# One joint run for the low-rank term of two groups, V0 in four quads, V loaded ahead of batch 1, and two x loads that wait for transposes

## The chip, the cores and the metric

The kernel runs on one core of a Trainium2 chip (trn2). The metric is the device time of one execution in microseconds. Three runs of the kernel before took 325.17, 325.19 and 325.78 us; their median is 325.19 us.

## The reference

The input x is (8, 4224, 192) in float32: 8 batches, 4224 positions, 192 channels. Two layers follow each other.

```
w   = softmax(weight)                       # 8 heads x 7 taps
y   = causal convolution of x with w        # 24 channels per head, 7 taps along the positions
h   = (y^T @ U @ V)^T                       # U: 4224 x 32, V: 32 x 4224, per batch
u   = y + h
out = u + relu(u @ w_ch1) @ w_ch2           # 192 -> 768 -> 192, per position
```

The product with U sums over all positions of a batch, so no position of a batch has its h before the batch's whole convolution is done.

## The kernel before

The 8 x 4224 positions are 264 tiles of 128, worked on in 33 **groups** of eight tiles. A batch has 33 tiles, so groups cross batches. The stages:

- **x loads.** `x_part` (L76) loads a quarter of a batch from GpSimd's queue (POOL in the profile) and converts it to bf16; `XP` (L84) names the quarters 0 to 3. Batch 0 comes in six pieces (`KP`, L86). x tiles have two buffers.
- **Convolution.** TensorE multiplies x with band matrices: `conv` (L355, matmuls L369) for batches 0 and 1, with the whole window in two halves, and `conv32` (L321, matmuls L339) for batches 2 to 7. The latter needs a shifted copy of x, `xb_sb` (one buffer), that POOL makes with the copies of `x_shift` (L286: L293, L295, L305). ACT and DVE evict the results to `y_sb` (L256, L258).
- **U.** `tt_mm` (L396, matmuls L402) forms y^T U; `tt_split` and `tt_sum` (L412, L425) bring the four partial sums together on all four row quarters, as `tt_sb`. For batch 0 the last tiles come in late by `tt_late` (L679, matmuls L682), which reads `U4_sb`, a copy that POOL makes (L701), and `tt_done` (L420) writes `tt_sb`.
- **h and u.** For groups from 2 on, `h_group` multiplies V with `tt_sb` (L457) and DVE adds y (L479) to `u_sb`; `transp` (L496) then transposes `u_sb` to `uT` with a DMA transpose on SP's queue (L498). `transp(3)` is held until the last matmul of the convolution of batch 1.
- **Groups 0 and 1** go without a DMA transpose: `yT_part` (L503, matmuls L509) transposes y on TensorE with the identity, straight into PSUM banks, and `hT_part` (L518, matmuls L524) adds h there, with `V0_sb` (32 rows, L132) as the moving operand; then ACT and DVE evict the banks to `uT` (L256, L258). h of group 0 comes first, then the rest of y^T of group 1, then its h.
- **The two layers.** `w1` (L542, matmuls L554) multiplies with `W1_sb`, with relu evictions on ACT (L568) and DVE (L570). `w2` (L577, matmuls L583) multiplies with `W2_sb`; DVE adds u (L592) and SP stores the result (L600).

Order of the work: the program is in the order in which it is written (`manual_schedule`), each engine takes its own instructions in that order, and waits for semaphores of the others. `SLOTS` (L619) is a list written out by hand: in each slot the W1 of some groups, then the pieces of W2 of some groups, with named steps at given pieces: `h3` (h of group 3, with its transpose), `d1` (convolution of batch 1), `c2:0:3:AAD` (three heads of the convolution of batch 2), `t1`/`s1` (the U product), `x2:6` (the six copies of `x_shift` for batch 2), `l2:3` (load of quarter 3 of batch 2, held until the last W2 piece issued so far). `LOADS` (L670) holds the other x loads until a given matmul of W1: `x_load` and `held` (L610, L602) add the wait. Since POOL is in order, what stands behind a held load on POOL waits with it. The built program gives POOL's loads eight semaphores in turn; a load waits until the load eight places before it on POOL has landed.

The order of POOL in the first 35 us: two x loads of batch 0, index patterns, U, two more x loads, V0, four loads of W1, quarter 0 of batch 1, the copy for `U4_sb`, five loads of V, W2, quarters 1 to 3 of batch 1, the copies for `band2`, then quarters 0 to 3 of batch 2.

Of the kernel before, what the change touches and what calls it, by code (L numbers as in the profile page):

```python
# [9 lines left out]
BF16 = mybir.dt.bfloat16  # L10
# [4 lines left out]
def kernel(  # L15
# [20 lines left out]
    GT = 8  # L36
# [3 lines left out]
    HB = P // 2  # L40
# [4 lines left out]
    cst = ctx.enter_context(tc.tile_pool(name="cst", bufs=1))  # L45
# [4 lines left out]
    uts = ctx.enter_context(tc.tile_pool(name="uts", bufs=5))  # L50
# [5 lines left out]
    def bank():  # L56
        return psp.tile([P, 512], F32, name="ps", tag="ps")
# [12 lines left out]
    def x_tile(b):  # L70
        xt[b] = xs.tile([P, NB1 + 1, D], BF16, name="x_sb")

    def x_zero(b, eng):
        eng.memzero(xt[b][0:HB, 0, :])

    def x_part(b, r, s0, s1):  # L76

        blk = NB0 * r + s0 - 1
        return nc.gpsimd.dma_start(  # L79
            out=xt[b][HB * r : HB * r + HB, s0:s1, :],  # L80
            in_=x[b, blk * HB : (blk + s1 - s0) * HB, :].rearrange("(j p) d -> p j d", p=HB),
        )

    XP = [(0, 1, 17), (0, 17, NB0 + 1), (1, 0, 18), (1, 18, NB1 + 1)]  # L84
# [18 lines left out]
    def iota(t, pattern, base, mul):  # L103
# [20 lines left out]
        out=Ur[:, 0:nfull, :], in_=U4[0 : nfull * P, :].rearrange("(k p) c -> p k c", p=P)  # L124
# [4 lines left out]
        x_piece(k)  # L129


    V0_sb = cst.tile([R, 2 * GT * P], BF16, name="V0_sb")  # L132
    nc.gpsimd.dma_start(out=V0_sb[:], in_=moe_V[:, 0 : 2 * GT * P])
    W1_sb = cst.tile([P, 3, M4], BF16, name="W1_sb")
    for m0, m1 in ((0, 2 * P), (2 * P, M4)):
        for hf in range(2):
            nc.gpsimd.dma_start(
                out=W1_sb[HB * hf : HB * hf + HB, :, m0:m1],
                in_=moe_w_ch1[:, m0:m1].rearrange("(c k) m -> k c m", k=HB),
# [27 lines left out]
    for hh in range(2):  # L167
# [3 lines left out]
        out=dif[:], in0=dif[:], scalar1=rq[:, 0:1], scalar2=None, op0=ALU.add  # L171
# [5 lines left out]
        out=d_sb[:],  # L177
# [8 lines left out]
        out=hot[:],  # L186
# [6 lines left out]
        out=ident[:], in0=fp[:], scalar1=float(P), scalar2=None, op0=ALU.is_equal  # L193
# [9 lines left out]
        out=c_sb[:].rearrange("p k h -> p h k"),  # L203
# [5 lines left out]
    for hh in range(2):  # L209
# [3 lines left out]
            out=pr[:],  # L213
# [8 lines left out]
        out=Eq[:], in0=efp[:], scalar1=rq[:, 1:2], scalar2=None, op0=ALU.is_equal  # L222
# [31 lines left out]
    def evac(eng, out, in_):  # L254
        if eng == "A":
            nc.scalar.activation(out=out, in_=in_, func=ACT.Copy)  # L256
        else:
            nc.vector.tensor_copy(out=out, in_=in_)  # L258
# [179 lines left out]
    uTt = [None] * NG  # L438
# [57 lines left out]
    def transp(g):  # L496
        uTt[g] = uts.tile([P, 4, 3, P], BF16, name="uT")
        return nc.sync.dma_start_transpose(  # L498
            out=uTt[g][:].rearrange("p i c t -> p (i c) t"),
            in_=ut[g][:].rearrange("p i c f k -> p (i c f k)"),  # L500
        )

    def yT_part(g, parts):  # L503


        for c, i0, i1, p, _ in parts:
            for i in range(i0, i1):
                for hf in range(2):
                    nc.tensor.matmul(  # L509
                        out=p[HB * hf : HB * hf + HB, (i - i0) * P : (i - i0 + 1) * P],  # L510
                        lhsT=yt[0][:, GT * g + 4 * hf + i, HB * c : HB * c + HB],
                        rhs=ident[:],
                        start=(i == i0),
                        stop=False,
                        tile_position=(0, HB * hf),
                    )

    def hT_part(g, parts):  # L518

        uTt[g] = uts.tile([P, 4, 3, P], BF16, name="uT")  # L520
        for c, i0, i1, p, _ in parts:
            for hf in range(2):
                t0 = (2 * g + hf) * 4 * P
                nc.tensor.matmul(  # L524
                    out=p[HB * hf : HB * hf + HB, 0 : (i1 - i0) * P],
                    lhsT=ttb[0][0:R, HB * c : HB * c + HB],
                    rhs=V0_sb[:, t0 + i0 * P : t0 + i1 * P],
                    start=False,
                    stop=True,
                    tile_position=(0, HB * hf),  # L530
                )
        for c, i0, i1, p, eng in parts:
            evac(
                eng,
                uTt[g][:, i0:i1, c, :],
                p[:, 0 : (i1 - i0) * P].rearrange("p (i t) -> p i t", t=P),
            )

    RELU = ["AD", "AD", "AA", "AD", "AD", "AD"]
    RELU0 = ["AA", "AD", "AA", "AD", "AA", "AD"]  # L540
# [77 lines left out]

    SLOTS = [  # L619
        ([0], [], {}),  # L620
        ([1], [0], {0: ["h0"], 1: ["h3", "l2:2"], 2: ["l2:3"]}),
        ([2], [1], {0: ["d1", "h1"], 1: ["t1"], 3: ["s1"], 4: ["h4", "x2:6"]}),
        ([3], [2], {1: ["h5"], 3: ["h6"]}),
        (
            [4, 5],
# [66 lines left out]
    work = [bank() for _ in range(4)]  # L692
    tp = bank()
    u_layout(work)
    x_tile(1)
    x_zero(1, nc.gpsimd)
    x_part(1, *XP[0])
    o = 0
    for r, (k0, k1) in KP[2].items():
        j = NB0 // 2 * r + k0  # L700
# [24 lines left out]
    W2_sb = cst.tile([P, MC, D], BF16, name="W2_sb")  # L725
    nc.gpsimd.dma_start(out=W2_sb[:], in_=moe_w_ch2[:].rearrange("(m p) d -> p m d", p=P))

    parts0 = [(0, 0, 2, bank(), "A"), (0, 2, 4, bank(), "D"), (1, 0, 4, bank(), "D")]
    yT_part(0, parts0)
    def conv_piece(k):  # L730
        for n, h in enumerate(range(0, H, 3)):
            for r in KP[k]:
# [6 lines left out]
    ps0 = work[3]  # L739
    for n, part in enumerate(ttb[0]):  # L740
        nc.tensor.matmul(out=ps0[:, 0:D], lhsT=R4[:], rhs=part[:], start=(n == 0), stop=False)
    more = [(2, 0, 2, bank(), "A"), (2, 2, 4, bank(), "A")]
    yT_part(0, more[0:1])
    tt_late(ps0)
    yT_part(0, more[1:])
    parts1 = [(0, 0, 4, bank(), "A")]
    yT_part(1, parts1)
    tt_done(0, ps0)
    hT_part(0, parts0 + more)
    rest = [(c, 0, 4, bank(), "ADA"[c]) for c in (1, 2)]  # L750
    yT_part(1, rest)
    hT_part(1, parts1 + rest)
    band2 = cst.tile([P, H, QB], BF16, name="band2")
    for xp in XP[1:]:
        x_part(1, *xp)
    for r in range(4):
        q = slice(QB * r, QB * r + QB)
# [6 lines left out]
    def do(what):  # L764
        if what[0] == "c":
            b, h0, n, engs = what[1:].split(":")
            conv32(int(b), int(h0), int(n), engs)
            return
        if what[0] == "d":
            for h in range(H):  # L770
                last = conv(int(what[1:]), h, 1, [0, 1], "AA" if h == 2 else "AD")
            held(transp(3), last)
            return
        if what[0] == "l":
            b, q = (int(v) for v in what[1:].split(":"))
            x_load(b, q, done_w2[-1])
            return
        if what[0] == "x":
            b, n = (int(v) for v in what[1:].split(":"))
            steps.extend(x_shift(b))  # L780
            for _ in range(n):
                steps.pop(0)()
            return
        n = int(what[1:])
        if what[0] == "h":
            h_group(n)
            if n > 1 and n != 3:
                transp(n)
        elif what[0] == "t":
            tt_split(n, tt_mm(n, range(NT)))  # L790
        else:
            tt_sum(n)
# [55 lines left out]
```

## Time and profile before

| | us |
|---|---|
| median of three runs | 325.19 |
| span of the profiled execution | 323.20 |
| PE busy | 317.6 |
| DVE busy | 268.6 |
| ACT busy | 170.0 |
| POOL busy | 142.7 |
| W1 of group 0 begins | 20.45 |
| W1 of groups 2 and 3 begins | 33.76, 47.12 |
| convolutions of batches 1, 2 and 3 begin | 37.75, 66.88, 95.08 |
| transposes of groups 2 and 3 issue | 27.14, 41.04 |

The span is the time from the first to the last instruction of the profiled execution; the median of the runs is 1.99 us above it. TensorE's granted clock is full from start to end. Times in the text are counted from the start of the span. A row of a timeline gives start, length, engine, line, operation and tiles, and in brackets how long the engine had been idle before it and what ended that. A row of the chain of waits gives start, length and what the chain ran through. "DMA to landing" is the time from the issue of a transfer to the semaphore that tells of its end; the three numbers are the least, the median and the most of the transfers asked for, and are equal for a single one.

### The profile page before, as it was taken

The page shows a single profiled execution, that of the slowest core. Times are in us where ns is not written, and L with a number is a line of the kernel's source. Part 1 is how long each engine was busy: PE and PEld are TensorE (multiplying, and loading weights), DVE is VectorE, ACT ScalarE, POOL GpSimd, SP SyncE. Part 2 cuts the span into 40 slices and gives each one's busy share as a digit, 9 for nine tenths or more (in the row PEclk, how much of TensorE's full clock was granted, in tenths as well). Part 3 has the DMA queues.
Part 4 walks back from the last instruction along what each step waited for, and adds up shares of the span by engine and source line. Part 5 has one row for each costly group of instructions (what it writes and reads, how often), then busy time and mean ns, then how long its engine had stood idle before and what let it go on. Part 6 is the DMA issues. An engine that isn't in the chain of part 4 may idle for free.

```text
span 323.2 us, 9583 instructions
## 1 busy us (share of the span) xinstructions
PE 317.6 (98%) x3996; PEld 223.7 (69%) x3996; DVE 268.6 (83%) x551; ACT 170.0 (53%) x344; POOL 142.7 (44%) x111
## 2 busy tenths in 40 slices
PE   8999999999999999999999999999999999999995
PEld 3747676478677647866864884687797497487495
DVE  6769989987977986997898699789888897896863
ACT  1766724860874397088239609824903902912910
POOL 8764179728957983992897497000000000000000
PEclk9999999999999999999999999999999999999999
DMA  9999993999998999599499957138268059048035
GB/s 106 192 191 183 206 209 100 196 192 257 208 135 200 246 142 190 166 189 209 130 237 192 181 149 194 52 105 231 61 178 262 3 150 275 18 121 271 2 121 173
DMA packets 122906, 53.51 MB, mean 166 GB/s; under 512 B 87760, under 2 KB 122832, under 8 KB 122864
## 3 DMA queue, kind: packets, MB, share of 16 engines
q1 hardware_dynamic: 84528, 38.08, 45.4%
q0 software_dynamic: 38192, 14.73, 39.2%
q8 instruction: 31, 0.51, 0.7%
q10 hardware_dynamic: 144, 0.10, 0.1%
q14 instruction: 11, 0.09, 0.1%
HBM read 29.49 MB, written 25.95 MB: 172 GB/s over the span
## 4 chain that ended last, share of the span: by engine, by line
PE 92%; ACT 3%; DMA 2%; DVE 1%; issue 0%; POOL 0%; POOLq 0%
PE ps L583 42%; PE ps L554 39%; PE ps L339 3%; PE ps L457 3%; DMA x_sb<-in_x_dram 2%; PE ps L402 2%; ACT rl_sb L568 2%; PE ps L369 1%; ACT y_sb L256 1%; PE ps L509 1%; DVE u_sb L479 1%; DVE rl_sb L570 1%; PE ps L524 0%; PE ps L428 0%; POOL x_sb L79 0%
## 5 line engine op out<-in xcount | busy, mean ns | idle before, releaser
L568 ACT ACTIVATE rl_sb<-ps 128x512 bf16<-128x512 f32 x233 | 124.3, 604 | 108.0 <-PE ps L554 96.0
L583 PE MATMUL ps<-W_sb,rl_sb 128*128 128x192 bf16 x1584 | 141.2, 246 | 0.2
L583 PEld LDWEIGHTS <-rl_sb 128*128 128x128 bf16 x1584 | 128.3, 98 | 11.8 <-issue 11.5
L554 PE MATMUL ps<-uT,W_sb 64*128 64x512 bf16 x1188 | 131.7, 376 | 0.0
L570 DVE TENSOR_SCALAR rl_sb<-ps 128x512 bf16<-128x512 f32 x163 | 105.3, 688 | 15.7 <-PE ps L554 15.4
L554 PEld LDWEIGHTS <-W_sb 64*128 64x128 bf16 x1188 | 66.9, 94 | 60.4 <-issue 3.9
L592 DVE TENSOR_TENSOR out_sb<-ps,u_sb 128x384 f32<-128x384 f32 (+1 forms) x133 | 70.4, 551 | 25.5 <-PE ps L583 25.0
L305 POOL COPY xb_sb<-x_sb 32x3072 bf16<-32x3072 bf16 (+1 forms) x24 | 67.4, 2824 | 0.5
L479 DVE TENSOR_TENSOR u_sb<-y_sb,ps 128x192 bf16<-128x192 bf16 (+1 forms) x168 | 66.3, 461 | 0.0
L293 POOL COPY xb_sb<-x_sb 128x3072 bf16<-128x3072 bf16 x12 | 32.7, 2742 | 42.1 <-PE ps L339 32.2
L256 ACT ACTIVATE y_sb<-ps 128x384 bf16<-128x384 f32 (+4 forms) x90 | 38.3, 520 | 9.7 <-PE ps L339 7.4
L79 POOL DMA_DIRECT2D x_sb<-in_x_dram x32 | 27.0, 848 | 9.6 <-PE ps L457 3.8
L258 DVE CAST y_sb<-ps 128x408 bf16<-128x408 f32 (+4 forms) x36 | 19.1, 578 | 1.3 <-PE ps L369 1.0
L457 PE MATMUL ps<-tt_sb,V_sb 32*128 32x192 bf16 x264 | 12.4, 246 | 0.1
L339 PE MATMUL ps<-x_sb,band 64*32 64x384 bf16 x192 | 12.1, 333 | 0.0
L339 PE MATMUL ps<-xb_sb,band 64*32 64x384 bf16 x192 | 12.1, 332 | 0.0
L457 PEld LDWEIGHTS <-V_sb 32*128 32x128 bf16 x264 | 4.7, 92 | 7.3 <-issue 7.3
L416 ACT ACTIVATE tt_hi<-ps 128x192 bf16<-128x192 f32 x8 | 2.6, 330 | 11.9 <-PE ps L402 11.9
L369 PE MATMUL ps<-x_sb,band 64*64 64x240 bf16 (+3 forms) x192 | 8.0, 276 | 0.2 <-DMA x_sb<-in_x_dram 0.2
L339 PEld LDWEIGHTS <-band 64*32 64x32 bf16 x384 | 4.5, 89 | 5.2 <-issue 2.4
L153 PE MATMUL ps<-zz 128*128 128x512 f32 (+1 forms) x10 | 6.7, 816 | 1.1 <-DVE zz L143 1.1
L369 PEld LDWEIGHTS <-band 64*64 64x64 bf16 x192 | 6.0, 106 | 2.1 <-issue 1.4
(65 smaller groups left out, 71.3 us busy)
## 6 DMA issues: line engine op xcount, KB each, us to landing
out_dram<-out_sb SPq DMA_DIRECT2D x131, 192.0 KB, 2.7
x_sb<-in_x_dram POOLq DMA_DIRECT2D x14, 384.0 KB, 6.9
x_sb<-in_x_dram POOLq DMA_DIRECT2D x7, 432.0 KB, 6.7
x_sb<-in_x_dram POOLq DMA_DIRECT2D x7, 408.0 KB, 8.0
x_sb<-in_x_dram POOLq DMA_DIRECT2D x1, 504.0 KB, 7.3
uT<-u_sb SPq DMA_TRANSPOSE x31, 3.5
x_sb<-in_x_dram POOLq DMA_DIRECT2D x1, 480.0 KB, 5.6
W_sb<-in_moe_w_ch_dram POOLq DMA_DIRECT2D x2, 192.0 KB, 7.8
```

What stands on the lines that cost most here:

```text
L79: return nc.gpsimd.dma_start(out=xt[b][HB * r : HB * r + HB, s0:s1, :], in_=x[b, blk * HB : (blk + s1 - s0) * HB, :].rearrange("(j p) d -> ...
L256: nc.scalar.activation(out=out, in_=in_, func=ACT.Copy)
L293: nc.gpsimd.tensor_copy(out=xbt[b][:, s0:s1, :], in_=xt[b][:, s0 + 1 : s1 + 1, :])
L305: nc.gpsimd.tensor_copy(out=xbt[b][q, s0:s1, :], in_=xt[b][q, s0:s1, :])
L339: nc.tensor.matmul(out=pp[r][QB * cg : QB * cg + QB, 0 : nk[r] * GS], lhsT=w[hr], rhs=t[hr, st : st + 2 * nk[r] - 1 : 2, hs], start=True, ...
L457: nc.tensor.matmul(out=banks[pr][:, a * D : (a + 1) * D], lhsT=V_sb[32 * q : 32 * q + 32, (j // 8) * 2 + j % 2, :], rhs=ttb[b][32 * q : 32 ...
L479: nc.vector.tensor_tensor(out=u_group(g)[:, i : i + n, :, hf, :], in0=yt[b][:, run[0] : run[0] + n, :].rearrange("p n (c k) -> p n c k", c=3),
L554: last = nc.tensor.matmul(out=pps[m][hf][:], lhsT=W1_sb[HB * hf : HB * hf + HB, c, m * P : (m + 1) * P], rhs=uTt[g][HB * hf : HB * hf + HB ...
L568: nc.scalar.activation(out=rl[:, m, hf, :], in_=pp[hf][:], func=ACT.Relu)
L570: nc.vector.tensor_scalar_max(out=rl[:, m, hf, :], in0=pp[hf][:], scalar1=0.0)
L583: last = nc.tensor.matmul(out=cps[:, a * D : (a + 1) * D], lhsT=rlt[g][:, m, hf, (i + a) * P : (i + a + 1) * P], rhs=W2_sb[:, m, :], start ...
L592: nc.vector.tensor_tensor(out=o[:, 0:n, :].rearrange("p n (c k) -> p n c k", c=3), in0=cps[:, 0 : n * D].rearrange("p (n c k) -> p n c k", ...
```

## The change

- `V0_sb` holds its 2048 columns as four quads of 512 on four row quarters, in four loads in place of one.
- y^T of groups 0 and 1 is laid out as one bank for each of the three channel parts (before, three parts were split in halves over two banks). All of y^T of both groups stands ahead of h, and `hT_part` takes both groups: for each channel part four matmuls, one on each row quarter.
- The allocation, memset and quarter 0 of batch 1 move behind V and W2 on POOL.
- Quarter 3 of batch 1 is held until the transpose of group 2 has landed; on POOL it stands behind the `band2` copies and ahead of batch 2.
- `l2:3`, the load of quarter 3 of batch 2, moves from the second slot's piece 2 to the third slot's piece 2, behind the convolution of batch 1 and the issue of the transpose of group 3.

```diff
-    V0_sb = cst.tile([R, 2 * GT * P], BF16, name="V0_sb")
-    nc.gpsimd.dma_start(out=V0_sb[:], in_=moe_V[:, 0 : 2 * GT * P])
+    V0_sb = cst.tile([4 * R, 4 * P], BF16, name="V0_sb")
+    for q in range(4):
+        nc.gpsimd.dma_start(
+            out=V0_sb[R * q : R * q + R, :], in_=moe_V[:, 4 * P * q : 4 * P * (q + 1)]
+        )
...
-    def hT_part(g, parts):
-
-        uTt[g] = uts.tile([P, 4, 3, P], BF16, name="uT")
-        for c, i0, i1, p, _ in parts:
-            for hf in range(2):
-                t0 = (2 * g + hf) * 4 * P
-                nc.tensor.matmul(
-                    out=p[HB * hf : HB * hf + HB, 0 : (i1 - i0) * P],
-                    lhsT=ttb[0][0:R, HB * c : HB * c + HB],
-                    rhs=V0_sb[:, t0 + i0 * P : t0 + i1 * P],
-                    start=False,
-                    stop=True,
-                    tile_position=(0, HB * hf),
+    def hT_part(of):
+
+
+        for c in range(3):
+            for g in range(2):
+                p = of[g][c][1]
+                for hf in range(2):
+                    q = 2 * g + hf
+                    nc.tensor.matmul(
+                        out=p[HB * hf : HB * hf + HB, :],
+                        lhsT=ttb[0][R * q : R * q + R, HB * c : HB * c + HB],
+                        rhs=V0_sb[R * q : R * q + R, :],
+                        start=False,
+                        stop=True,
+                        tile_position=(R * q, HB * hf),
+                    )
+        for g in range(2):
+            uTt[g] = uts.tile([P, 4, 3, P], BF16, name="uT")
+            for c, p, eng in of[g]:
...
-        ([1], [0], {0: ["h0"], 1: ["h3", "l2:2"], 2: ["l2:3"]}),
-        ([2], [1], {0: ["d1", "h1"], 1: ["t1"], 3: ["s1"], 4: ["h4", "x2:6"]}),
+        ([1], [0], {0: ["h0"], 1: ["h3", "l2:2"]}),
+        ([2], [1], {0: ["d1", "h1"], 1: ["t1"], 2: ["l2:3"], 3: ["s1"], 4: ["h4", "x2:6"]}),
...
     u_layout(work)
-    x_tile(1)
-    x_zero(1, nc.gpsimd)
-    x_part(1, *XP[0])
...
-    parts0 = [(0, 0, 2, bank(), "A"), (0, 2, 4, bank(), "D"), (1, 0, 4, bank(), "D")]
-    yT_part(0, parts0)
+    parts0 = [(c, bank(), "ADA"[c]) for c in range(3)]
+    yT_part(0, parts0[0:2])
...
-    more = [(2, 0, 2, bank(), "A"), (2, 2, 4, bank(), "A")]
-    yT_part(0, more[0:1])
+    yT_part(0, parts0[2:])
     tt_late(ps0)
-    yT_part(0, more[1:])
-    parts1 = [(0, 0, 4, bank(), "A")]
+    parts1 = [(c, bank(), "ADA"[c]) for c in range(3)]
     yT_part(1, parts1)
     tt_done(0, ps0)
-    hT_part(0, parts0 + more)
-    rest = [(c, 0, 4, bank(), "ADA"[c]) for c in (1, 2)]
-    yT_part(1, rest)
-    hT_part(1, parts1 + rest)
+    hT_part([parts0, parts1])
     band2 = cst.tile([P, H, QB], BF16, name="band2")
-    for xp in XP[1:]:
+    x_tile(1)
+    x_zero(1, nc.gpsimd)
+    for xp in XP[:3]:
         x_part(1, *xp)
...
             if n > 1 and n != 3:
-                transp(n)
+                last = transp(n)
+                if n == 2:
+                    held(x_part(1, *XP[3]), last)
```

More of the change, by code (lines that the diff above doesn't have):

```diff
@@ L503, in yT_part @@
     def yT_part(g, parts):
-        for c, i0, i1, p, _ in parts:
-            for i in range(i0, i1):
+        for c, p, _ in parts:
+            for i in range(4):
                 for hf in range(2):
                     nc.tensor.matmul(
-                        out=p[HB * hf : HB * hf + HB, (i - i0) * P : (i - i0 + 1) * P],
+                        out=p[HB * hf : HB * hf + HB, i * P : (i + 1) * P],
                         lhsT=yt[0][:, GT * g + 4 * hf + i, HB * c : HB * c + HB],
                         rhs=ident[:],
-                        start=(i == i0),
+                        start=(i == 0),
                         stop=False,
@@ L516, in yT_part @@
                     )
-    def hT_part(g, parts):
-        uTt[g] = uts.tile([P, 4, 3, P], BF16, name="uT")
-        for c, i0, i1, p, _ in parts:
-            for hf in range(2):
-                t0 = (2 * g + hf) * 4 * P
-                nc.tensor.matmul(
-                    out=p[HB * hf : HB * hf + HB, 0 : (i1 - i0) * P],
-                    lhsT=ttb[0][0:R, HB * c : HB * c + HB],
-                    rhs=V0_sb[:, t0 + i0 * P : t0 + i1 * P],
-                    start=False,
-                    stop=True,
-                    tile_position=(0, HB * hf),
-                )
[L532 to L537, printed above, removed]
+    def hT_part(of):
[15 more added lines that the diff above has]
+            for c, p, eng in of[g]:
+                evac(
+                    eng,
+                    uTt[g][:, :, c, :],
+                    p[:].rearrange("p (i t) -> p i t", t=P),
+                )
     RELU = ["AD", "AD", "AA", "AD", "AD", "AD"]
```

## The prediction

> **What bounds the kernel now.** I read the page first: PE is busy for 317.6 of 323.2 us at full clock. Then I compared PE's runs of equal matmuls with the shortest run of the same kind in this trace: all excess together is 5.85 us, 2.8 of it between 20 and 80 us. So TensorE's own work is the time, little can be won, and anything that makes TensorE wait is paid in full. Second, the chain of waits from 15 to 48 us:
>
> ```profile
> PE 317.6 (98%) x3996; PEld 223.7 (69%) x3996; DVE 268.6 (83%) x551; ACT 170.0 (53%) x344; POOL 142.7 (44%) x111
> ...
> 18.35 0.83 PE ps L524 x10
> 19.18 0.57 PE ps L509 x16
> 19.75 0.76 PE ps L524 x6
> 20.51 1.23 PE ps L554 x10
> 21.74 3.04 ACT rl_sb L568 x6
> ...
> 35.92 2.54 ACT rl_sb L568 x5
> 38.47 3.10 ACT y_sb L256 x8
> ```
>
> Two places are not TensorE's: ACT's relus from 21.74, and its relus and convolution evictions up to 41.56. Third, POOL's timeline (start, length, line), and fourth, the time from issue to landing of single transfers (transposes first issued at 27.1, 41.0, 49.5 and 67.3, then x loads at 22.1, 30.1, 64.2 and 91.3):
>
> ```profile
> 11.38 0.63 POOL L137 DMA_DIRECT2D W_sb<-in_moe_w_ch_dram  x1 [0.88 <-DMA Ur<-in_moe_U_dram]
> 13.27 0.82 POOL L701 COPY U_sb<-U_sb 128x768 bf16<-128x768 bf16 x1 [0.31 <-ACT U_sb L256]
> 45.35 2.74 POOL L293 COPY xb_sb<-x_sb 128x3072 bf16<-128x3072 bf16 x1 [1.41 <-DMA x_sb<-in_x_dram]
> 60.11 1.63 POOL L79 DMA_DIRECT2D x_sb<-in_x_dram  x2
> 74.89 2.74 POOL L293 COPY xb_sb<-x_sb 128x3072 bf16<-128x3072 bf16 x1 [0.84 <-DMA x_sb<-in_x_dram]
> 88.32 3.08 POOL L305 COPY xb_sb<-x_sb 32x3456 bf16<-32x3456 bf16 x1
> ...
> DMA to landing us min/median/max: 5.1/5.1/5.1
> DMA to landing us min/median/max: 5.6/5.6/5.6
> DMA to landing us min/median/max: 3.2/3.2/3.2
> DMA to landing us min/median/max: 8.3/8.3/8.3
> ...
> DMA to landing us min/median/max: 8.8/8.8/8.8
> DMA to landing us min/median/max: 7.0/7.0/7.0
> DMA to landing us min/median/max: 10.5/10.5/10.5
> DMA to landing us min/median/max: 5.6/5.6/5.6
> ```
>
> A transpose takes 3.2 us alone and 5.1 to 8.3 beside x loads; an x load 5.6 in a quiet queue and up to 10.5 (12.6 for the one of 32.7) in a full one. POOL is strictly in order: the two L293 copies wait for the last quarter of x.
>
> **The base.** The span is 323.20 us; the median of the three runs is 325.19, so 1.99 us lie around it. I add my sum to both alike.
>
> **1. The joint run.** PE's matmuls of L524 start 0.216 us apart in pairs (six in 0.83). Before, the h of group 0 starts at 18.34, when DVE has written `tt_sb`, and W1 at 20.45. After, all 24 identity matmuls of group 1 stand ahead of h: 16 of them took 0.57, at 0.053 per further pair, so 24 take 0.78, from 17.82 to 18.60. DVE's wait up to 18.34 is thus filled. Then 12 h matmuls on four row quarters. That four run at once is shown by the h run at 24.44 (L457, eight on four row quarters, each 0.25, in 0.34 together), so three sets of 0.216. Channel part 0 ends at 18.97, ACT evicts it in 0.54 (two of 512 columns took 1.08) to 19.55, W1 starts at about 19.65, and its second tile waits for DVE's copy (0.69) to 19.9. ACT then has three more evictions, to 21.2, and only then the relus: they start at 21.2, not 21.73. Since ACT's relus end this stretch, the gain is **-0.53**, though W1 starts 0.8 earlier. Four quarters not running at once would cost 3 x 0.216 = 0.65 more.
>
> **2. V0 in four quads.** Three more issues on POOL, each about 0.55 (L133 took 0.56). The built program gives POOL's loads eight semaphores in turn, so a load waits until the one eight before it has landed; the row at 11.38 is such a wait (on `Ur`). Three loads more shift the pairing: the W1 loads now wait for `Ur` (11.1) and the late x pieces (landed 12.9, 14.5). The last W1 load issues at 14.74 instead of 11.38, the U4 copy follows from 15.4 to 16.25 instead of 13.27. TensorE first uses that copy at 16.90 (L682): cover 0.6. The last W1 load is used from 21.1. The queue moved 185 to 195 GB/s without a pause from 4 to 29 us, with the same bytes ahead of it; that lands it at about 18.9, as before. By its own row of 7.5 it would land at 22.3, **+1.2**. V follows at 16.3 to 18.7, W2 at 19.3 (needed 28.7). V by its last row (6.5 from 18.1) lands at 24.6, 0.7 after h of group 2 wants it; by the queue's rate at 21. I take nothing for this step: the queue is the limit and has no more to move. Bounds 0 and +1.2.
>
> **3. Batch 1 behind V, its last quarter behind the transpose of group 2.** The three free quarters now issue at 20.3 to 22.9; the fourth, before issued at 22.1 (landing 8.8 later, 30.9), waits at the head of POOL until that transpose has landed. The transpose issues at 27.14 - 0.53 = 26.6; by 5.1 it lands at 31.7 (bounds 3.2 and 8.3: 29.8, 34.9). The third quarter is still in flight then, so I take 5.1. Add 0.3 from landing to issue (as between 11.10 and 11.38), and 5.6 to 8.8 for the load; nearest is the 7.0 of the load of 30.1, a neighbour in time, though with another ahead of it, so I take the middle of 5.6 and 7.0: 31.7 + 0.3 + 6.3 = 38.3. Convolution d1 would start at 37.75 - 0.53 = 37.2 and wait 1.1. ACT hides some: its first eviction came 0.72 after d1's start, and one head takes 0.33 plus 0.1, so 0.3 is spare. Cost **+0.75**; bounds 0 (29.8 + 5.9 = 35.7) and +6.5 (34.9 + 0.3 + 8.8 = 44.0). Behind the waiting load on POOL stand a memset and the first three quarters of batch 2, which go from 29.3 to about 33.
>
> The Trainium skill, "DMA: Bandwidth & Descriptors", section "Anatomy of one DMA — SWDGE (gpsimd) path", fits a load from GpSimd as 2.0 us plus bytes over 436 GB/s. As an estimate from that page the 408 KB would land in 3.0 us, at 35.0, and this step would cost nothing. The quietest x load of this trace took 5.6, so I stay with the rows.
>
> **4. The transpose of group 3.** It issues behind d1, at 41.04 + 0.2 = 41.25. It took 5.6 beside one x load. Now about three quarters of batch 2 are under way, as with the 8.3 at 67.3 (two under way). Middle 7.0: landing 48.2, and W1 of group 3 is due at 47.12 + 0.2. Cost **+0.9**, bounds 0 and +2.2. That the last quarter of batch 2 no longer runs beside it speaks for the low end.
>
> **5. The last quarter of batch 2.** It now waits for the second W2 piece of group 1, which ends at 44.7, so it issues at 44.9 instead of 32.7. Queued behind it on POOL are all x2 copies. By 7.2 (middle of 5.6 and 8.8) it lands at 52.1, where before it landed at 45.3. From there to the end of the copies is 59.99 - 45.35 = 14.6: 66.7. Convolution c2 (66.88) comes at 68.0: covered by 1.3; by 12.6 us of load it would cost 4.1. But the x3 loads stand behind these copies: 66.9 instead of 60.1, the last at 69.4, and by 10.5 it lands at 79.9. From that landing to the end of the x3 copies is 91.4 - 74.9 = 16.5: 96.4. Convolution c3 (95.08) is due at 96.2. Cost **+0.2**, bounds 0 and +3.6 (rival B). After c3 a batch needs about 25 of its 27 us, so nothing is carried on.
>
> Sum: -0.53 + 0.75 + 0.9 + 0.2 = +1.3; 323.2 becomes 324.5 in the span, and the time **326.5 us**.
>
> **Rivals.**
> A, all waits are covered, so not slower: the waiting transfers run in quiet queues. The held quarter takes 5.6 (37.6, within ACT's 0.3), the transpose 5.6 (46.6, before 46.6 to 47.1), the last quarter of batch 2 5.6 (50.0, copies end 64.6), x3's last lands at 77.8 (copies end 94.3, c3 due at 94.6). Only step 1 is left: **324.7**. For it speaks that each transpose is freed of one load; it decides where the held quarter lands by 37.5. Chance 0.28.
> B, the chain of x overtakes: POOL's copies, 14.6 and 16.5 us after a late last quarter, make c3 wait. With 8.8 for the held loads (x2's lands at 53.7, copies end 68.3, x3's last issue 71.0) and 10.5 to 12.6 for x3's last, the copies end at 98.0 to 100.1 against 96.5: 2.9 to 5.0 in all, **329**. For it: out stores from 70 us on share the engines. Against: before, 3.7 us of cover stood here. Chance 0.18.
> C, the eight semaphores bite in the prologue (W1 or U4 late): +1.2 in place of -0.53, later waits partly absorbed, about **327**. Chance 0.06.
> D, the joint run is not four wide: -0.53 becomes about 0, **327.1**; the change then does not do what it says. Chance 0.04.
>
> **Numbers.** Forecast (steps 1 to 5 as taken, 325.5 to 327.5) 0.44, A 0.28, B 0.18, C 0.06, D 0.04. A measurement of this kernel can tell about 0.2% (0.65 us) from no change: 324.54 to 325.84. A's lower part, 0.12, is faster; its rest and the low end of the forecast (0.16 + 0.09) are the same; the remaining 0.63 is slower. The range leaves out about 0.1 on each side: 324.5 (below A, little is to be gained) to 329.2 (B's middle; beyond lie 8.8 and 12.6 us loads together).
>
> **What will show it.** Step 1: relus of L575 starting near 21.2. Step 2: the L685 run still near 16.9, no DMA wait ahead of W1 of group 0. Step 3: a wait on x ahead of d1 near 37.2. Step 4: a wait on the transpose ahead of W1 of group 3. Step 5: POOL's x2 copies ending near 66 and any wait on POOL ahead of c2 or c3. I am wrong if the held loads land in under 6 us each (A), or if the convolutions c2 and c3 wait by microseconds (B).

## The result, and the profile after

The changed kernel takes 343.81 us (median of six runs, 338.09 to 345.0), the kernel before 325.18 in the same session. By these medians it is slower by 18.6 us. The ratio, 1.046 [1.039, 1.053] or 14.9 us, leaves out the four runs over 1.5% above the fastest (343.63 to 345.0, the profiled one among them), so that a difference below that starts from 343.81 is uncertain by some 4 us. The forecast was 326.5, its range ended at 329.2. The sign was right and the size was not. The profiled execution took 345.0 us; its span is 343.22 us, 20.0 more than before.

The page of the changed kernel, instructions and granted clock:

```profile
PE 321.4 (94%) x3992; PEld 225.6 (66%) x3992; DVE 269.3 (78%) x550; ACT 170.2 (50%) x343; POOL 144.4 (42%) x114
...
PEclk9999989999996699999999999999999999999999
```

PE is busy 3.8 us longer than before, with four instructions fewer, and the span grew by 20.0. So some 16 us are idle time of TensorE; and its clock, full throughout before, now falls in slices 6, 13 and 14 of 40 (8.6 us each), which fits that fewer instructions are busy for longer. The waits of PE (engine, line and what it waited for; us in all, how often, the longest):

```profile
PE ps L342 <- POOL xb_sb L308: 10.3, 3, 7.3
PE ps L372 <- DMA x_sb<-in_x_dram: 3.9, 2, 3.5
PE ps L561 <- DMA uT<-u_sb: 2.3, 2, 1.4
```

All three are of the kinds that the prediction named: c2 and c3 (the convolutions of batches 2 and 3) on POOL's copies, d1 (that of batch 1) on an x load, W1 on a transpose. Where they stand is in PE's timeline; the row by itself is d1 in the kernel before, without a wait:

```profile
37.75 3.24 PE L369 MATMUL ps<-x_sb,band 64*64 64x384 bf16 x64
```

```profile
18.77 0.84 PE L529 MATMUL ps<-V_sb,tt_sb 32*64 32x512 bf16 x12
...
34.20 4.06 PE L561 MATMUL ps<-uT,W_sb 64*128 64x512 bf16 x36 [0.91 <-DMA uT<-u_sb]
...
41.99 4.41 PE L372 MATMUL ps<-x_sb,band 64*64 64x408 bf16 x62 [3.46 <-DMA x_sb<-in_x_dram]
...
96.54 4.06 PE L561 MATMUL ps<-uT,W_sb 64*128 64x512 bf16 x36 [1.44 <-DMA uT<-u_sb]
105.01 0.48 PE L342 MATMUL ps<-xb_sb,band 64*32 64x384 bf16 x1 [2.32 <-POOL xb_sb L308]
112.75 0.49 PE L342 MATMUL ps<-xb_sb,band 64*32 64x408 bf16 x1 [7.27 <-POOL xb_sb L308]
```

Setting the starts of W1 of the same group side by side tells where the 20 us came in:

| W1 of group | before | after | shift |
|---|---|---|---|
| 0 | 20.45 | 19.89 | -0.56 |
| 1 | 24.83 | 24.29 | -0.54 |
| 2 | 33.76 | 34.20 | +0.44 |
| 3 | 47.12 | 52.31 | +5.19 |
| 5 | 60.34 | 65.52 | +5.18 |
| 6 | 81.09 | 87.09 | +6.00 |
| 8 | 88.87 | 96.54 | +7.67 |
| 9 | 109.39 | 129.64 | +20.25 |
| 32 | 303.75 | 323.98 | +20.23 |

Two places make nearly all of it: the stretch with d1 (between groups 2 and 3, +4.75) and the stretch with c3 (between 8 and 9, +12.58). Everything is lost before 130 us; after that nothing is won back and nothing more is lost. POOL's timeline shows where both begin (x1, x2 and x3 below are the loads of batches 1, 2 and 3):

```profile
34.68 0.89 POOL L79 DMA_DIRECT2D x_sb<-in_x_dram  x1 [9.93 <-DMA uT<-u_sb]
...
50.75 0.89 POOL L79 DMA_DIRECT2D x_sb<-in_x_dram  x1 [12.54 <-PE ps L590]
...
73.23 3.36 POOL L79 DMA_DIRECT2D x_sb<-in_x_dram  x4
92.86 2.74 POOL L296 COPY xb_sb<-x_sb 128x3072 bf16<-128x3072 bf16 x1 [16.27 <-DMA x_sb<-in_x_dram]
```

The first two rows are the held quarters; the brackets say that POOL stood still for 9.93 and 12.54 us ahead of them. The four loads of batch 3, issued before from 60.11 to 65, now go out at 73.23 to 76.6, and POOL then stands still for 16.27 us before the first copy that needs them. Issue to landing, from the view of transfers: the transpose of group 2, the held quarter of batch 1, the transpose of group 3, the last load of batch 3:

```profile
uT<-u_sb SPq DMA_TRANSPOSE x1, 7.5
...
x_sb<-in_x_dram POOLq DMA_DIRECT2D x1, 408.0 KB, 7.2
...
uT<-u_sb SPq DMA_TRANSPOSE x1, 3.9
...
x_sb<-in_x_dram POOLq DMA_DIRECT2D x1, 408.0 KB, 20.4
```

### The profile page after: what moved, and what is told of

It reads as the page before. It is cut to its first block, busy times and chain, and to the rows that moved or that the text cites. A ratio compares the mean times of both kernels' runs of the same rounds, so it can differ in the third digit from the quotient of the medians.

```text
span 343.2 us, 9575 instructions
## 1 busy us (share of the span) xinstructions
PE 321.4 (94%) x3992; PEld 225.6 (66%) x3992; DVE 269.3 (78%) x550; ACT 170.2 (50%) x343; POOL 144.4 (42%) x114
## 4 chain that ended last, share of the span: by engine, by line
PE 69%; DMA 13%; POOL 10%; issue 5%; DVE 1%; ACT 1%; POOLq 0%
PE ps L590 32%; PE ps L561 29%; DMA x_sb<-in_x_dram 10%; POOL xb_sb L308 7%; PE ps L342 3%; DMA uT<-u_sb 2%; POOL x_sb L79 2%; PE ps L460 2%; POOL xb_sb L296 2%; PE ps L405 1%; PE ps L372 1%; ACT y_sb L259 1%; DVE u_sb L482 1%; DVE rl_sb L577 0%; PE ps L512 0%
## 5 line engine op out<-in xcount | busy, mean ns | idle before, releaser
L575 ACT ACTIVATE rl_sb<-ps 128x512 bf16<-128x512 f32 x233 | 124.3, 605 | 110.1 <-PE ps L561 98.2
L590 PE MATMUL ps<-W_sb,rl_sb 128*128 128x192 bf16 x1584 | 142.7, 248 | 0.0
L342 PE MATMUL ps<-xb_sb,band 64*32 64x384 bf16 (+1 forms) x192 | 13.8, 356 | 10.3 <-POOL xb_sb L308 10.3
L372 PE MATMUL ps<-x_sb,band 64*64 64x240 bf16 (+4 forms) x192 | 9.4, 308 | 4.0 <-DMA x_sb<-in_x_dram 3.9
L342 PE MATMUL ps<-x_sb,band 64*32 64x384 bf16 x192 | 13.0, 357 | 0.0
L372 PEld LDWEIGHTS <-band 64*64 64x64 bf16 x192 | 7.5, 115 | 5.5 <-issue 4.7
```

The source lines that it names most:

```text
L342: nc.tensor.matmul(out=pp[r][QB * cg : QB * cg + QB, 0 : nk[r] * GS], lhsT=w[hr], rhs=t[hr, st : st + 2 * nk[r] - 1 : 2, hs], start=True, ...
L575: nc.scalar.activation(out=rl[:, m, hf, :], in_=pp[hf][:], func=ACT.Relu)
L590: last = nc.tensor.matmul(out=cps[:, a * D : (a + 1) * D], lhsT=rlt[g][:, m, hf, (i + a) * P : (i + a + 1) * P], rhs=W2_sb[:, m, :], start ...
```

## The experiments

My theory after the result: the holds cost nearly all, the second above all, by a late x chain on POOL; the joint run itself gives its half microsecond. The first rival: the three more loads of V0 and the new order of POOL's loads cost by themselves, whatever is held. Four kernels take the change apart.

**The joint run alone.** The changed kernel with batch 1 in its old place and neither hold:

```diff
-                last = transp(n)
-                if n == 2:
-                    held(x_part(1, *XP[3]), last)
+                transp(n)
...
+        ([1], [0], {0: ["h0"], 1: ["h3", "l2:2"], 2: ["l2:3"]}),
```

> Of the change only V0 in four quads and the joint run; batch 1, V and both last quarters as before. Theory (the joint run gains what its step said, all the loss is in the held loads): ACT's relus of group 0 start near 21.2 as in the changed kernel, and the time is 0.5 below before, 324.7 (324.4 to 325.0). Rival (the three loads more on POOL cost later what the joint run gains): 325.2 or more, with a wait on a load between 20 and 40 us.

Measured: 329.64 against 325.04, ratio 1.012 [1.008, 1.016]. The theory's figure fell: without any hold the joint run costs 4.6 us in the median. The lead of step 1 is there (W1 of group 1 at 24.40, before 24.83), and is gone at group 2. The chain of waits of this kernel:

```profile
26.71 7.94 DMA uT<-u_sb
34.70 4.06 PE ps L561 x36
...
41.98 6.36 DMA uT<-u_sb
48.38 4.08 PE ps L561 x36
```

Before, the same transposes took 5.1 and 5.6 us and nobody waited for them. Now both set the start of W1 (34.70 and 48.38; before 33.76 and 47.12). So the wait of the rival is there, though on transposes and not on a load. The profiled run is the fastest of the six (327.13, the others reach 333.32) and shows 2.4 of the 4.6 us, W1 of group 9 at 111.77 in place of 109.39; what makes the others slower is not shown.

**Joint run and V ahead of batch 1, neither hold.** The changed kernel with all four quarters of batch 1 in one loop behind V:

```diff
-    for xp in XP[:3]:
+    for xp in XP:
         x_part(1, *xp)
...
-                last = transp(n)
-                if n == 2:
-                    held(x_part(1, *XP[3]), last)
+                transp(n)
...
+        ([1], [0], {0: ["h0"], 1: ["h3", "l2:2"], 2: ["l2:3"]}),
```

> The changed kernel without the two holds: V stays ahead of batch 1, quarter 3 of batch 1 follows quarter 2 at once, quarter 3 of batch 2 is back in its old slot. Theory (the holds carry the loss): convolution of batch 1 starts without a wait near 37.2 to 38, the time is 324.7 to 326.5; the transpose of group 2 may come 0 to 2 us late, because quarters 2 and 3 of batch 1 run beside it. Rival (the order V before batch 1 starves the transfers and is itself the loss): over 329, with the wait for x ahead of d1 still there.

Measured: 332.48, ratio 1.023 [1.021, 1.024], 2.8 above the joint run alone: over 329, as the rival had it, but d1 waits only 0.2 us. The wait, of 4.99 us, is ahead of W1 of group 2. Its transpose is issued at 26.18, with all four quarters of batch 1 behind V in its way:

```profile
26.18 11.63 DMA uT<-u_sb
37.81 0.05 issue
37.85 6.34 PE ps L561 x36
```

The granted clock is half from 35.60 to 42.42. Where the delay comes from is seen earlier, in what the transfers move. Windows of the kernel before, then of the changed kernel (busy time of PE, PEld, DVE, ACT and POOL, the granted clock, share and GB/s of the transfers):

```profile
16.00:18.00 2.00, 1.78 (x30) 1.07 (x26) 0.68 (x2) 0.71 (x2) 0.73 (x2) 1.00 1.33 197
18.00:20.00 2.00, 2.00 (x42) 1.34 (x40) 1.31 (x3) 1.04 (x3) 1.91 (x3) 1.00 1.56 191
20.00:22.00 2.00, 2.00 (x22) 0.76 (x20) 0.93 (x2) 1.35 (x3) 0.78 (x2) 1.00 1.47 186
```

```profile
16.00:18.00 2.00, 1.85 (x36) 1.19 (x30) 0.77 (x2) 0.88 (x2) 2.00 (x5) 1.00 1.08 151
18.00:20.00 2.00, 1.72 (x39) 1.14 (x40) 0.93 (x2) 0.76 (x2) 2.00 (x5) 1.00 1.08 138
20.00:22.00 2.00, 2.00 (x20) 1.41 (x18) 1.49 (x4) 2.00 (x5) 2.00 (x4) 1.00 0.68 62
```

The last column is the reading: (46 + 53 + 124) GB/s for 2 us each are 446 KB not moved, 2.3 us of the queue at its 190 GB/s, and about one quarter of batch 1 (408 KB). POOL is busy for all of these 6 us: its waits on the semaphores come before (the last W1 load goes out at 14.90, before at 11.38), and then it issues load after load, too late to keep the queue full. In the kernel without holds the three windows show 159, 129 and 75 GB/s, and its fourth quarter of batch 1 lands at 34.24, before at 30.91: here the missing bytes run beside the transpose.

**The first hold alone** (joint run, V ahead, the last quarter of batch 1 held; `l2:3` in its old place). Against the changed kernel:

```diff
-        ([1], [0], {0: ["h0"], 1: ["h3", "l2:2"]}),
-        ([2], [1], {0: ["d1", "h1"], 1: ["t1"], 2: ["l2:3"], 3: ["s1"], 4: ["h4", "x2:6"]}),
+        ([1], [0], {0: ["h0"], 1: ["h3", "l2:2"], 2: ["l2:3"]}),
+        ([2], [1], {0: ["d1", "h1"], 1: ["t1"], 3: ["s1"], 4: ["h4", "x2:6"]}),
```

> The changed kernel with quarter 3 of batch 2 back in its old slot; only quarter 3 of batch 1 is held. Theory (each hold costs its own wait): convolution of batch 1 waits about 3.5 us and runs at half clock as in the changed kernel, W1 of group 3 near 52, and c3 does not wait by more than 1 us, because x3's loads go out as early relative to the matmuls as before: 329 to 331. Rival (the first hold alone already pushes POOL's chain so that c3 waits): over 335.

Measured: 331.07, ratio 1.017 [1.014, 1.020], 1.4 below the kernel without holds. So the first hold helps a little: the transpose lands at 33.47 (without it, at 37.81), the held quarter at 42.05, and the wait moves from W1 of group 2 to d1 (4.32 us). It moves a loss of this size; it doesn't make it. And c3 doesn't wait, as the theory had it: the first hold alone doesn't push POOL's chain that far.

**The second hold alone** (joint run, V ahead, `l2:3` in the third slot, batch 1 not held). Against the changed kernel:

```diff
-    for xp in XP[:3]:
+    for xp in XP:
         x_part(1, *xp)
...
-                last = transp(n)
-                if n == 2:
-                    held(x_part(1, *XP[3]), last)
+                transp(n)
```

> The changed kernel with quarter 3 of batch 1 loaded at once; only quarter 3 of batch 2 is held. Theory (this hold makes POOL's copies and then the loads of batch 3 late, which meet the stores): x2 copies end 65 to 67, loads of batch 3 go out near 67 and take up to 20 us, c3 waits 5 to 10 us and the granted clock falls behind it: 333 to 340. Rival (c3's wait is a consequence of d1's delay): under 328.

Measured: 346.23, ratio 1.065 [1.064, 1.067], 13.7 above the kernel without holds and above the 333 to 340 expected. Its x2 quarter goes out at 53.24, the x3 loads at 76.09 to 78.5, the last of them takes 19.5 us. TensorE's waits:

```profile
PE ps L342 <- POOL xb_sb L308: 10.7, 3, 7.4
PE ps L561 <- DMA uT<-u_sb: 7.1, 2, 6.4
...
PE ps L372 <- DMA x_sb<-in_x_dram: 0.3, 1, 0.3
```

c3 waits as long as in the changed kernel (the longest wait is 7.4, there 7.3), with next to no wait ahead of d1, so the rival is out. Taken in a row, from the kernel before by the joint run alone, neither hold and the first hold to the changed kernel, the steps are 4.6 us for the joint run with its loads, 2.8 for V ahead, -1.4 for the first hold, and 343.81 - 331.07 = 12.7 for the second on top of the first (by the ratios 3.8, 3.5, -2.0 and 9.5). These steps add up to the whole by construction; in another order they may differ, as the second hold does without the first. By medians and by ratios the second hold is the greatest part.

**Are the 4.6 us in the number of loads?** Two kernels. One is the kernel before with nothing but V0 in four loads:

```diff
-    nc.gpsimd.dma_start(out=V0_sb[:], in_=moe_V[:, 0 : 2 * GT * P])
+    for q in range(4):
+        nc.gpsimd.dma_start(
+            out=V0_sb[:, 4 * P * q : 4 * P * (q + 1)], in_=moe_V[:, 4 * P * q : 4 * P * (q + 1)]
+        )
```

> The kernel before, with nothing changed but that V0 comes in four column pieces (four loads) instead of one; h is as before. Theory (three loads more shift the pairing of POOL's eight semaphores, POOL falls behind, and the transfer queue runs dry for about 1 us before 24 us): the queue moves under 160 GB/s somewhere between 16 and 24 us, quarter 3 of batch 1 lands near 31.8 instead of 30.9, the transpose of group 2 lands at 34 to 35 and W1 of group 2 waits about 1 us: 326.5 to 330. Rival (the joint run is what makes the transpose late in the run with it alone): 325.0 to 325.5, transpose near 32.3 as before.

The other is the joint run alone with W1 in two loads in place of four, so that only one load is added:

```diff
-    for m0, m1 in ((0, 2 * P), (2 * P, M4)):
+    for m0, m1 in ((0, M4),):
         for hf in range(2):
```

> The run with the joint run alone, with the four loads of W1 joined to two, so that POOL has one load more than before instead of three. Theory (the number of loads, not the joint run, costs): the queue has no gap of more than 0.3 us, the transpose of group 2 lands by 33, and the time falls to 324.6 to 326. Rival (the joint run itself, or the order, costs): like the run with four W1 loads, 327 to 330.

Measured: 326.12, ratio 1.003 [1.002, 1.005], and 326.45, ratio 1.004 [1.002, 1.006]. Three more loads with no other change cost 1.0 us, less than expected (326.5 to 330): the queue moves 164, 183 and 161 GB/s in the three windows, the last x1 load lands at 32.91 (before 30.91), and the transpose of group 2 joins the chain of waits:

```profile
27.28 6.96 DMA uT<-u_sb
```

(W1 of group 2 follows at 34.28, 0.52 later than before. 0.13 of this is older: TensorE waited 0.4 us for the late U4 copy in the prologue, the thing that step 2 had looked for.)

With W1 in two loads the queue shows no gap (200, 192 and 190 GB/s in the three windows), the last x1 load lands at 30.75, and the joint run costs 1.3 in the median in place of 4.6. So the number of loads is the greater part of the 4.6 us, but only together with the joint run: alone it costs 1.0. But it doesn't win its half microsecond either: the transpose is issued at 26.52, 0.6 earlier than before, takes 7.19 us, lands at 33.71, and W1 of group 2 starts at 33.76, to the hundredth where it started before. My expectation that it would land by 33 failed. This trace is of a run of 324.75 us and has W1 of group 9 at 109.38, as before (109.39); the 1.3 us of the median are in the other runs (up to 328.65), of which there is no trace.

**What hides the joint run's gain, then?** Four kernels in which the transposes are plain copies of the same bytes between the same tiles: the kernel before, the changed kernel, the joint run with W1 in two loads, and this last one with 58 more TensorE instructions in the prologue, which move TensorE's instruction fetch (it falls beside the transposes, see the last section) to an earlier time.

```diff
-        return nc.sync.dma_start_transpose(
-            out=uTt[g][:].rearrange("p i c t -> p (i c) t"),
+        return nc.sync.dma_start(
+            out=uTt[g][:].rearrange("p i c t -> p (i c t)"),
```

In the last one also (the idle matmuls of the prologue in bf16, and more of them):

```diff
-    zz = cst.tile([P, P], F32, name="zz")
+    zz = cst.tile([P, P], BF16, name="zz")
...
-    idle(4)
+    idle(27, 4)
...
-    idle(1, 2)
+    idle(3, 4)
```

> The kernel before, with each DMA transpose of u to uT replaced by a plain DMA copy of the same 384 KB on the same queue (uT is then not transposed, so the output of groups 2 to 32 is another one; all waits are the same). It gives the base for the next three. Theory (the kernel before is bound by TensorE, its transposes are covered): 324.9 to 325.4. Rival (transposes already cost something there): under 324.5. The copy of group 2 lands within 3 to 4.5 us of its issue.

> The kernel with the joint run and W1 in two loads, with plain copies instead of DMA transposes. Theory (the landing of the transpose of group 2 ate the 0.55 us that the joint run gained): W1 of group 2 begins near 33.2 and the time is 0.4 to 0.6 under that of the kernel before with copies. Rival (the gain is lost elsewhere): equal to it within 0.2.

> The changed kernel with plain copies instead of DMA transposes, as above. Theory (the hold of quarter 3 of batch 1 costs through the slow end of the transpose that it waits for; the hold of quarter 3 of batch 2 costs by itself): the copy of group 2 lands near 30.5 instead of 34.15, quarter 3 of batch 1 near 38 instead of 41.9, d1 waits under 1 us and keeps full clock, while c3 still waits 5 us or more: 331 to 338. Rival (the holds are too late whatever they wait for): d1 waits 2 us or more also here, 338 to 344.

> The kernel with the joint run, W1 in two loads and plain copies, with 58 instructions more on TensorE at the start (idle matmuls in bf16 instead of float32, the same 6 us). Theory (an instruction fetch of TensorE beside a transfer holds up its landing): the fetch near 31 moves by 2 us or more, and the landing of the copy of group 2 changes by 0.5 us or more against the run without the shift. Rival (the fetch is only queued with the rest): landing within 0.3 us of that run; the time equal within 0.3 us in either case.

Measured, in this order. Before with copies: 325.00, ratio 0.999 [0.998, 1.001]; the copy of group 2 takes 4.95 us (27.27 to 32.22), and as W1 starts at 33.89 it was covered, as the transpose was. The joint run with copies: 323.96, ratio 0.996 [0.994, 0.999]; the copy lands at 32.52, W1 of group 2 starts at 33.10 without a wait. The two rows, before with copies first:

```profile
33.89 2.33 PE L554 MATMUL ps<-uT,W_sb 64*128 64x512 bf16 x20
```

```profile
33.10 3.20 PE L561 MATMUL ps<-uT,W_sb 64*128 64x512 bf16 x28
```

The 0.79 us are still there at group 32 (303.87 and 303.08), and the medians differ by 325.00 - 323.96 = 1.0 us, more than the 0.4 to 0.6 expected. So the joint run gains once nothing waits for a transpose; it is the transpose's landing that takes it. (For the 33.76 with a transpose the profile names an eviction of DVE that ends at 33.75; with copies W1 starts before the same eviction ends, so that isn't what holds it.) The changed kernel with copies: 341.10, ratio 1.046 [1.040, 1.051]. PE's timeline:

```profile
39.70 3.04 PE L372 MATMUL ps<-x_sb,band 64*64 64x408 bf16 x62 [2.14 <-DMA x_sb<-in_x_dram]
...
107.69 0.50 PE L342 MATMUL ps<-xb_sb,band 64*32 64x408 bf16 x1 [7.42 <-POOL xb_sb L308]
```

The copy landed at 32.32, 1.8 earlier than the transpose, and still d1 waits 2.14 and c3 7.42: the holds are too late whatever they wait for, as the rival had it. The fourth: 326.54, ratio 1.004 [1.001, 1.006], and inconclusive. The fetch moved from 30.08 to 29.10, not by the 2 us planned, and the copy took 3.57 in place of 6.03, but the prologue became longer as well (W1 of group 0 at 21.57, without the added instructions 19.77), so that fewer x loads ran beside the copy. For a real transpose nothing was measured: three kernels planned for it, two that move the fetch and one with half of W2 to load, gave no result.

**Why does the second hold cost 13 us?** Theory: the x3 loads now run among the output stores; rival: the x chain is as late by its start alone. The changed kernel without the stores of groups 3 to 5:

```diff
+        if g in (3, 4, 5):
+            return
```

> The changed kernel, with the stores of groups 3, 4 and 5 left out (those rows of the output are not written). Theory (the loads of batch 3, late by 13 us, meet these stores on the engines and take 20 us instead of 10): the last of them lands within 9 to 12 us of its issue, c3 waits under 3 us instead of 10, and the time is 331 to 335. Rival (the loads are slow by themselves, or c3 waits because POOL's copies start late): still over 340.

Measured: 335.03, ratio 1.030 [1.027, 1.032], 8.8 less than the changed kernel (by the ratios 5.3). The last x3 load, issued at the same time (75.72), takes

```profile
x_sb<-in_x_dram POOLq DMA_DIRECT2D x1, 408.0 KB, 10.4
```

where it took 20.4 with the stores. c3 waits 1.93 us in place of 9.6 (2.32 and 7.27), and W1 of group 9 starts at 119.19, 10.5 earlier. The meeting with the stores is the greater part of the second hold's price; the rest, which the late start leaves, wasn't taken apart further.

**What does the half clock cost?** The changed kernel with idle matmuls ahead of d1 (4) and of c3 (11), which keep TensorE busy in the waits; `warm(n)` issues n float32 matmuls of the zeros in `zz`, 512 columns each, into a bank of their own:

```diff
+        if what[0] == "d":
+            warm(4)
...
+            if (b, h0) == ("3", "0"):
+                warm(11)
```

> The changed kernel with idle matmuls on TensorE ahead of the convolutions of batch 1 (4 of 0.8 us) and batch 3 (11 of 0.8 us), where it would stand idle for 3.5 and about 10 us. Theory (the half clock of 3.4 and 13.6 us follows from the idle time and costs about half of those stretches in which TensorE works): the granted clock stays at full speed and the time falls by 3 to 6 us, to 335 to 340, the waits themselves staying. Rival (the clock falls for another reason, or costs nothing beside the waits): within 2 us of the changed kernel, 339 to 345.

Measured: 341.24, ratio 1.049 [1.047, 1.051], 2.6 below the changed kernel. The windows around c3, first of the changed kernel, then of this one:

```profile
105.00:118.00 13.00, 5.73 (x66) 3.25 (x66) 2.65 (x5) 3.15 (x8) 9.22 (x7) 0.50 0.95 102
```

```profile
99.00:112.00 13.00, 12.85 (x76) 6.54 (x73) 2.32 (x5) 1.26 (x4) 12.83 (x9) 1.00 0.65 91
```

The clock is 1.00 in place of 0.50 (the PE column now holds idle matmuls and says nothing), and c3 still has to wait for POOL's copies, until 111.19. So the half clock follows from the waits and isn't their cause. Its price can be read from the traces: from d1's first long run to W1 of group 3 it takes 10.32 us in the changed kernel and 9.32 here (before 9.37), from the release of c3 to W1 of group 9 16.89 and 14.37 (before 14.38). These are 1.0 and 2.5 us. In the time itself a gain isn't shown: the medians differ by 2.6 (341.24 lies outside the 335 to 340 expected), but the changed kernel's runs reach from 338.09 to 345.0, and the intervals of the two ratios overlap.

## Why the prediction was wrong, step by step

**The bound** was read rightly: TensorE is the time, and the waits put before it were paid. 16 of the 20 us of the profiled execution are its idle time.

**Step 1** held: relus of L575 at 21.16 (forecast 21.2), 12 h matmuls in 0.84, four side by side, and W1 of group 1 earlier by 0.54 (forecast 0.53). W1 of group 0 came earlier by 0.56, where 0.8 was forecast. Rival D is out. In ACT's timeline:

```profile
21.16 3.57 ACT L575 ACTIVATE rl_sb<-ps 128x512 bf16<-128x512 f32 x7
```

**Step 2** failed in its last sentences, "I take nothing for this step: the queue is the limit and has no more to move". I had looked for a late W1 or a late U4 copy; neither came (last W1 load in time, V by 22.0, L689 at 17.07). What came was a starved queue: I had counted the bytes and not when POOL could issue them. With 446 KB too little by 22 us, the quarters 0 to 2 of batch 1 land at 26.57, 28.59 and 31.05, the times at which the quarters 1 to 3 landed before (26.08, 28.45 and 30.91): batch 1 is behind by one quarter. Where that quarter isn't held, it runs beside the transpose, which takes 11.63. The price isn't seen in the prologue but at the first thing that shares the engines with what was put off. Taken 0; the experiments put the joint run with three more loads at 4.6 us and V ahead at 2.8 when nothing is held.

**Step 3** had the right mechanism and the right place, and both its terms too small. The transpose took 7.54 (taken 5.1, bound 8.3) and gave W1 of group 2 a wait of 0.91, which I hadn't put down. The held quarter went out 0.53 after the landing (taken 0.3) and took 7.18 (taken 6.3, bound 8.8): 41.86 in place of 38.3. Of the 3.6 us by which it landed later, 2.4 are the transpose, 0.9 the load and 0.2 the issue, so the row of 5.1, taken for a transpose beside loads, was the choice that failed most. Why the transpose took 2.4 us longer than before isn't shown: the three x loads beside it land nearly as three did before. d1 waited 3.46, and the whole stretch cost 4.75, taken 0.75, bound 6.5; 1.0 of it is the half clock, which the sum didn't hold.

The page that I had set against the rows, the Trainium skill's "DMA: Bandwidth & Descriptors", would have put the held load at 3.0 us; the run shows 7.2, and the rows were the better guide, though the value taken from them was still too low.

**Step 4** erred to the other side: the transpose of group 3 took 3.87 (taken 7.0) and cost nothing (taken 0.9). With d1 so late, two of the three x2 loads of 35.73 to 38.2 had landed (43.93 and 45.97) before it was issued at 46.44; the third landed at 49.06.

**Step 5** is the step that failed most. Its chain was right, link by link: landing to the end of the copies took 14.7 (taken 14.6) and 16.6 (taken 16.5), and "after c3 nothing is carried on" holds (+20.25 at group 9, +20.23 at group 32). The two transfers at its ends were mis-sized. The held quarter went out at 50.75, not 44.9. The W2 piece that it waits for ended at 49.88, before at 44.70, since it stands behind d1, and d1 was late: step 3's loss came back here as an input, 5.18 where the sum carried 0.2. From that piece's end to the issue another 0.87 passed (0.81 before), which the sum had left out. It landed at 58.34 (52.1 taken). The x3 loads followed at 73.23 (66.9), and the last took 20.38, where 10.5 was taken and 12.6 the most I had seen: 96.06 in place of 79.9. Copies end at 112.7 (96.4), and c3, due at 102.7, was fully released at 112.75. Taken 0.2, bound 3.6; measured 12.58 (9.59 of it waits of c3, 2.5 the half clock), with 0.81 more at c2 and 1.67 ahead of W1 of group 8, where transposes met the same x loads. Rival B was this very mechanism, and its 10.5 and 12.6 came from loads that overlapped six and five output stores; the load of 75.68 overlapped eleven, one or more of them at every moment. I had written of "out stores from 70 us on" and had not asked what a load costs that runs wholly among them. The experiment without stores shows it: 10.4 again.

**What no step held** is the clock. Around the waits of 3.46 and 7.27 us TensorE ran at half speed; by the traces that cost 1.0 and 2.5 us. The windows (granted clock third from the end):

```profile
38.00:42.00 4.00, 0.54 (x8) 0.14 (x5) 1.01 (x2) 0.90 (x2) 0.21 (x1) 1.00 1.52 177
42.00:47.00 5.00, 5.00 (x73) 3.71 (x74) 3.96 (x8) 3.82 (x9) 0.00 (x0) 0.66 1.42 169
...
105.00:118.00 13.00, 5.73 (x66) 3.25 (x66) 2.65 (x5) 3.15 (x8) 9.22 (x7) 0.50 0.95 102
```

The Trainium skill, "TensorE: Matmul & The Clock Gate", section "Part 1: The HAM clock gate", says that an idle window of about 3.4 us brings TensorE back to half clock. The run agrees in the length: after d1's wait the half clock lasts 3.41 us (43.31 to 46.73), though it begins only 1.3 us after work has resumed at 41.99. It doesn't agree that a wait must be that long: at c3 the clock falls at 104.75, when TensorE had been idle for 2.07 us, and after the wait of 2.14 us ahead of d1 in the changed kernel with copies it stays full. So no single length of wait decides here, and the sum should have held a possible addition for waits from about 2 us on.

Measured by places, the shift of the table is -0.54 (group 1), +0.98 (group 2), +4.75 (d1), +0.81 (c2), +1.67 (group 8) and +12.58 (c3), 20.25 in all.

What stays open: why the transpose of group 2 takes 7.2 to 7.9 us in the two joint runs and in the changed kernel, when the x loads beside it land nearly as before; and why the joint run's times spread (327.13 to 333.32, with W1 in two loads 324.73 to 328.65), those of the kernel before mostly from 324.8 to 325.8. No version here with its transposes is faster than the kernel before; the 1.0 us of the joint run was seen only with copies.

## What to carry to other kernels

A load that is held until an event costs more than its own wait when it stands in an ordered queue: follow everything behind it to its next use, and price the transfers by what runs beside them at their new time, not by the row from their old time. Steps that are late feed each other (here d1 set when the second hold ended, and this set when loads met stores), so a sum of independent terms came out too low; redo it with each loss put in. And splitting a small load is not free because its bytes are the same: count the issues, and see whether the queue stays full.

## What was not expected of the hardware

- A load that takes 10.4 us beside no stores takes 20.4 among them (issued at 75.72 and 75.68, 408 KB, three like it ahead).
- A transpose of the same size took 3.2 us with no x load beside it, 4.8 to 8.3 beside x loads in the first 70 us before, 11.63 and 13.07 in the two kernels with V ahead and without the first hold. Plain copies in its place behave alike: 2.53 with no x load, 3.57 to 6.11 beside loads for groups 2 and 3.
- Between the issue and the landing of the transpose of group 2 a fetch of TensorE instructions (16 KB, 0.9 to 1.2 us) runs in each of these four traces: at 29.04 before with the landing at 32.27, at 30.76 with W1 in two loads (33.71), at 31.66 in the joint run (34.65), at 31.62 after (34.15). That the one causes the other is not shown; the attempt to shift the fetch changed the loads as well.
- The half clock comes in stretches of 3.41 us or twice, three or four times that: 3.41 at d1 in the changed kernel, 6.83 without holds, 10.24 around c3 with copies, 13.65 around c3 in the changed kernel (104.75 to 118.41). In the last, c3 was released at 112.75, and the clock came back only after 5.7 us of nearly unbroken work.
